# Another order table for a two-block attention and two-expert kernel: the same instructions in another order, some on other engines

## The chip, the cores and the metric

The kernel runs on one core of one Trainium2 chip. The metric is device time in microseconds (us) of one execution. Engines are named as in the profile: PE is TensorE (matmuls; PEld its weight loads), DVE is VectorE, ACT is ScalarE, POOL is GpSimd, SP is SyncE, which issues most DMAs.

## The reference

Rotary attention over 4 batches of 8 heads, 576 positions and 64 columns, and two dense expert layers on the 2304 resulting rows of 512 columns:

```python
q_rot, k_rot = (rotate(q), rotate(k))
scores = scale * np.matmul(q_rot, k_rot.transpose(0, 1, 3, 2))
scores = scores - np.max(scores, axis=-1, keepdims=True)
attn = np.exp(scores)
attn = attn / (np.sum(attn, axis=-1, keepdims=True) + 1e-09)
x = np.matmul(attn, v)                     # to 2304 x 512
...
h = x @ w_in                               # first expert layer, 512 -> 2048 -> 512
g = h * np.clip(h + 3.0, 0.0, 6.0) / 6.0
x = g @ w_out
...
h = x @ w_in                               # second expert layer
P = a[0] + a[1] * h + a[2] * h2 + a[3] * h3
Q = 1.0 + np.abs(b[0]) * np.abs(h) + np.abs(b[1]) * h2
out = (P / (Q + 1e-06)) @ w_out
```

## The kernel before

**Numbers.** Operands of matmuls are split into two 16-bit halves: an upper half (a cast, possibly with a scale) and a lower half (the rest that the cast left off). A product takes three matmuls, upper by upper, upper by lower and lower by upper. So nearly every operand costs a cast and a subtraction or a fused multiply and subtract. Float32 weights are first decoded from the raw bytes (L422 to L427), squared and summed for a scale (L442, L453), and then split (`split16`, L433 and L434, for the first expert; `split_w2`, L1052 and L1053, for the second, whose halves are written over the tile of the weight before them, so that the cast of one weight waits for the second half of the last).

**Attention.** 16 head pairs P0 to P15, four for each batch. `prep_qk` rotates q and k: two products with the sine table (L640), one in place with the cosine table over 1280 columns (L647), two sums (L657), the casts (helper `copy`, L311 on ACT, L313 on POOL, L315 or L317 on DVE) and lower halves (L671), and a DMA transposition (tile `qkt`). A `unit` is 128 rows of queries of both heads of a pair, or the last 64: scores on PE (L704 to L715, tile `s` in PSUM), their row maximum (L719, DVE), a small scalar (L725 or L727), the exponential on ACT (L736), the upper half of P (L757, through `copy`) and the lower half (L758), a DMA transposition, and the product with v on PE (L794).

**First expert.** `layer1` takes 256 rows of one batch at a time, or the 4 x 64 rows left over: PE into PSUM (L899), a gate on ACT and DVE (L906, L908), the upper half of g (`gh`, L910, through `copy`) and the lower (`gl`, L912), and the second matmul (L927).

**Second expert.** `layer2` takes blocks of 512 rows and two of 128 columns of h at a time: PE fills one of two PSUM tiles, `hh` or `hx` (L1151). ACT reads it three times (L1177, L1178, L1179) and DVE twice (L1183, L1184). A chain of further instructions on tiles `lq`, `ls`, `lt` and `lr` gives P / Q, its halves are `lgh` (L1192, ACT) and `lgl` (L1193, DVE), and PE multiplies them with w_out (L1203) into four PSUM tiles `ac`.

**What sets the order.** The function does not emit instructions as it runs: each call of `op` appends an operation with its dependences to a list of 3527, and `Plan.order` then reads the table `ORDER`, a compressed list of numbers. Each number names an operation, the engine that runs it (`"PADGQN"`: PE, ACT, DVE, GpSimd, the SP queue, none) and one of two PSUM banks. Operations are emitted in exactly this order, so each engine's queue, which runs in order, is a subsequence of the table, and semaphore waits between the engines follow from the dependences and from who uses a tile first. The list of engines and the costs given to `op` are not read when a table is there:

```python
for x in code:
    o, e = self.ops[x // 12], "PADGQN"[x % 12 // 2]
    if o.need is not None:
        o.need.bank = x % 2
    ...
    done.add(o.idx)
    result.append((o, e))
```

Of the kernel before, what the change touches and what calls it, by code (L numbers as in the profile page):

```python
# [32 lines left out]
KF = DFF // 128  # L33
# [67 lines left out]
    'PXqjv<`X4ky{$}|ZO2xVXBfA<gSM{FUX01S>FBr3Z<t@8aVTWFAo&~2MWrs-^)r<WD>Io5xu48rbQtsK(3vsh0_$2%o2BE*7jip<@q9~W9^LY^',
    'LWxz$W|fo~%|v7!7RZcNYK{ms5QM6P!G=5qF#G1<hheBqmw6gJy=LL@=?`M6!2;|D=G&f1HUXgo?vc~wK6b8Vx|9&~(;aqE4O<cUu@#e}iTj=%',
    'L_;Y%X*va=kEYlNJW7XQ($g)UIo7d1lo|2O*cSqo9}dGKyG446+5MjUM`_&}dSgAgAqC;CwIhdM$FCpMS(~_eC>>)48$guZ&l#}%aGQ-CkN#p9',
    '&!%I1>gB=U$j@5*W4LEUV3w^OL>b_DXW=vK^MR>@+bo3WDX|KGX9nJEiN6T+#dYX2NAv1nKHeTUb1?6Z9`wQ(>xFu=1K&B`>Y$Hlp9sMZ_C81M',
    'vr^3U*O+L95YLllgX~B2&k#RMu;b9fc5|vQCOSMeLvNnJNb2z3hxu^*c-}7xJ(tZbsl^V%bJ+)<3YNw@OdZCRyO{ZD#E}kn^ZMyUw8qyvAC0|H',
    'dbq*X#Jb(QV7I9&EpW-af(SdK38_ok6MNI7-g<}Mdr#!=A0^-N8AhYFkkp|9cFPOj*EGxCqLN(<v))Kb(F{C)CV5ZOpf&jrzqKS&n#wk89cIK{',
    '$iSX;URX^V@}eAsdc&jmpi8_;rdbzkTS56g-hW()%FPh8b|oDy(FWlJU4dR0g*xL4%D;*2P8j{@G2`A{`z*xGN4iDpK{w`owTQb7`IPn81pS3u',
    '>gd+GHzxeZ&4FEe(yUN=l@|8gtxUBk@0l^L29>E>dNV6BhV|=*psXnGntv#**tL=$RAmd#H!ro&+LRw!l>#MUHYx4qj#;8KDP=Te7b`p(Bj&ho',
    '-rTi1klQAe-vA%PL|#YNVO{C8VzkhX@+fB}lyWfSCTp3^df(aCU`#vhybzzuL;F+-niKlpSw5)uTGkySt_*k`>zQZgP?86&h#6P<B}rE8GS60q',
    'zs8YIi#!{w0_`>$Ivo9l<+xaCpZ2_@{bY_s;J7j93&Ct=!n^2p;9a$v4*g`9e&4dK=f1G%|K&Oja^-jFkC7uZ(r7P8M)I}AO06e3C|9eUv>!P3',  # L110
    'PBTCJJ^hk!<M6q@LIzVh<SNC&b=FA>$*S8U)lwDK=<fk%mM@y`vtDl#T_V?0aizdqS1OUeLvRh2a=SlXN#x~pu~Wh;H<qbTLL^07#Ywbx%QHka',
    'UG<ISpEqkYY|359-0`YtZ7?<99c6E(zst^RyU9LnCK>Twr5D&Uf%}<D2K<fty>KNM`S_IB=AOt5X}tb4Hwe?nPc7^+-0-Q0nY>H|oPi6TD?%ZS',
    'rx!gM{26-t9ms+9w4^Qxk>oGbPp4n9&HNn}{&<G0yZxDYCio(3!0jXtVa*L8zxrXzb29S@%(Ndm5#4#gQ+s(N<Zh9+^t4)>?(*~r7gO)48Pc8P',
    'NcbJRvr*NdH|>WGE$H824-@NdIQ`1og*?_nLeT6l{UA@<a8@!aYLry5Qei5a*Luy5{L*-!K?us|3b`Z=TcxSK&`M(4?Fw8<`0?tcU_-nUd*35=',
    '9#@p-OvYDJ6`|lkEOi#~jf@7Rht<-zEsxv_!&XtCj4j6tgl8g;(0sftu&K@n%h}zoSx0#<^}jr@qz!c|d7qq$A6@&A_DyLaUKTv3wkF1Mwhw~v',
    'fADoFrmiIPU*QOSl^V16_Xlt7U-nHIgZbUbUN~aIG<F<G3qn&G*u2+Bb+9#iD<_p|fo*Rv6@vdp{Ljl>R0owv$iQdqhsXL8Yqkc*(c+H$$JYDo',
    'ZTX5-j{CI9SvIm}<au@x8j+u;#8RgbuN5mQYlQ);TfSq(%sTx??mr7_ZVBn3<0O{lkek50X-9vDJVTkUncqd$Jpt9C1D*D?n1QI>DLu5$p{HOi',
    '*i<gUs1!>Jq}+<JMoALR$TLQvG-Fq3pG^7SCA%Swle2QndM=ixI;DEGCLJXsxF*Uve5=M;pAL%#vZOD8QFu4==icIkf!A(k`t1Slf7v<EXFc&2',
    'I&pD9sz|MQrVrP0=2L_A>!^N3{-VNbuL;g0I|kt#AYKsHx6MM5&6V~q=6~|a$+;n9_NTQbF-SSv-@#Qq;vKVF8MA6^KSXIr85bkSWbM94d^V8p',
    '8mymvnf^@B(CU0@K+T7HnO;i*Be3BtzM*}n5>=|AzfJ#DI?oE6#9`E@N^S8(fbXi1uQ>mNnZKH2urYc|>Sih#WmhrNI(*CizR>1k$HLldbBCco',  # L120
    'm~!8iu(t*7{gki$EcT?lw+gXd<IWPhD9pOe__}zQ3sd@<ID_3eMxQ6Ev{Z77X;1{Wd>X2izjCWGo5*<0So@l<7v`LYqG^8~DuoG`cVw<QB&_w{',
    '$65nDdRPP})p{6DcdK*k0zAg*UQKu8FMr$wi|Gb6Ec`9J%g!X{-`Zh%e8YK=mVCL%qt#PdlUvIAGppVjvO@D{5DLW=T0?4K)(F4#Z2K`@SCe;q',
    '@1Z`38@Ig;sY&0kk?)He9H-pEtd^Us_HkaaXjkCLeq*u%F+2Ln(N`yY{V<%ZwXslTJW3+TN#A8-HFWNScePI^>+~q?l*+ZW#6Y%ULU4h#1s)#o',
    'Pou2USPwLKcN6c^PqQfLh229Ps)B3#ItZVfOEq~ThpVC=2AE_0G$#P%=_>5cC&(o>!k(#-4`xGZqTXMT4#9EX^tKFt;_H_)bj*$#OTMwd;zvcu',
    'uf4!=*Ch9tN7ySw?L1-zA&5w8kQ+Ts@G_m{Rd3-d{`<zUioK^HKg5w&>)9-7u@P2GsJSZ@+d*R@&>gSHoup5(dl&B+`ARYrPX$)UC$P@TWM1V@',
# [1184 lines left out]
```

## Time and profile before

| | |
|---|---|
| time, three runs | 1069.85 us median (1069.81 to 1078.24) |
| the profiled execution | 1069.65 us, of which the span of instructions is 1067.9 us |
| PE busy | 971.1 us, 91% of the span |
| DVE busy | 908.9 us, 85% |
| ACT busy | 738.2 us, 69% |
| POOL busy | 186.2 us, 17% |

The profile is of one execution. Busy times are unions of the engine's instructions; a group's mean is that of its instructions' durations. A stretch of the span is given in us from its start. What an instruction waited for is inferred from semaphore events. Line numbers are those of the kernel before; in the changed kernel they are one higher, as the table has one line more.

### The profile page before, as it was taken

The page shows a single profiled execution, that of the slowest core. Times are in us where ns is not written, and L with a number is a line of the kernel's source. Part 1 is how long each engine was busy: PE and PEld are TensorE (multiplying, and loading weights), DVE is VectorE, ACT ScalarE, POOL GpSimd, SP SyncE. Part 2 cuts the span into 40 slices and gives each one's busy share as a digit, 9 for nine tenths or more (in the row PEclk, how much of TensorE's full clock was granted, in tenths as well). Part 3 has the DMA queues.
Part 4 walks back from the last instruction along what each step waited for, and adds up shares of the span by engine and source line. Part 5 has one row for each costly group of instructions (what it writes and reads, how often), then busy time and mean ns, then how long its engine had stood idle before and what let it go on. Part 6 is the DMA issues. An engine that isn't in the chain of part 4 may idle for free.

```text
span 1067.9 us, 20042 instructions
## 1 busy us (share of the span) xinstructions
PE 971.1 (91%) x7978; PEld 686.2 (64%) x7978; DVE 908.9 (85%) x1389; ACT 738.2 (69%) x1144; POOL 186.2 (17%) x165
## 2 busy tenths in 40 slices
PE   1358799999999999999999989988999999999998
...
PEclk9997799999999999999999999999999999999999
...
GB/s 263 251 223 200 93 120 130 171 152 154 139 162 169 157 147 141 164 106 150 145 80 207 235 165 115 21 40 0 40 41 40 1 39 2 11 1 50 1 20 40
DMA packets 253853, 117.04 MB, mean 110 GB/s; under 512 B 223552, under 2 KB 241088, under 8 KB 253760
## 3 DMA queue, kind: packets, MB, share of 16 engines
...
## 4 chain that ended last, share of the span: by engine, by line
PE 41%; DVE 15%; ACT 7%; issue 3%; POOL 1%; ACTq 0%; DVEq 0%; POOLq 0%
PE h L927 10%; PE ac L1203 10%; PE h L899 8%; PE hx L1151 4%; PE hh L1151 4%; PE h L794 3%; DVE lt L1183 2%; PE s L704 1%; DVE lt L1184 1%; DVE lq L1188 1%; DVE lt L1189 1%; DVE lt L1191 1%; DVE lgl L1193 1%; ACT ls L1178 1%; ACT lq L1177 1%
## 5 line engine op out<-in xcount | busy, mean ns | idle before, releaser
L899 PE MATMUL h<-xt,w 128*128 128x256 f16 x1728 | 199.2, 274 | 5.4 <-DVE t L908 2.8
L927 PE MATMUL h<-gh,w 128*128 128x256 f16 x1080 | 189.1, 273 | 0.0
L899 PEld LDWEIGHTS <-w 128*128 128x128 f16 x1728 | 168.6, 99 | 26.6 <-issue 6.5
L927 PEld LDWEIGHTS <-w 128*128 128x128 f16 x1620 | 156.6, 98 | 18.3
L1203 PE MATMUL ac<-w2o,lgh 128*128 128x512 f16 x516 | 153.4, 379 | 0.5 <-ACT lgh L1192 0.5
L1151 PEld LDWEIGHTS <-w2i 128*128 128x128 f16 x900 | 87.8, 98 | 98.5 <-issue 7.9
L927 PE MATMUL h<-gl,w 128*128 128x256 f16 x540 | 147.2, 273 | 0.0
L736 ACT ACTIVATE e<-s,mx,qal 128x576 f32<-128x576 f32 (+1 forms) x144 | 115.7, 831 | 14.8 <-POOL mx L727 6.1
L719 DVE TENSOR_REDUCE mx<-s 128x2 f32<-128x1152 f32 (+1 forms) x80 | 99.0, 1242 | 5.7 <-PE s L707 4.8
L1151 PE MATMUL hh<-x,w2i 128*128 128x512 f16 (+1 forms) x468 | 100.3, 359 | 2.8 <-DVE y1m L1083 1.4
L1203 PE MATMUL ac<-w2o,lgl 128*128 128x512 f16 x258 | 97.8, 379 | 1.1 <-DVE lgl L1193 1.1
L1151 PE MATMUL hx<-x,w2i 128*128 128x512 f16 (+1 forms) x432 | 91.0, 357 | 6.3 <-DVE lt L1184 3.3
L1203 PEld LDWEIGHTS <-lgh 128*128 128x128 f16 x544 | 53.1, 98 | 64.0 <-issue 1.2
L906 ACT ACTIVATE t<-h,half,d 128x512 f32<-128x512 f32 (+1 forms) x96 | 61.5, 667 | 43.1 <-PE h L899 33.1
L758 DVE TENSOR_TENSOR p<-e,p 128x1152 f16<-128x1152 f32 (+1 forms) x63 | 79.8, 1267 | 7.2 <-ACT p L311 6.1
L794 PE MATMUL h<-v,pt 128*128 128x130 f16 (+3 forms) x1440 | 75.5, 207 | 8.9 <-DVE t L908 3.2
L794 PEld LDWEIGHTS <-pt 128*128 128x128 f16 (+1 forms) x1440 | 71.7, 100 | 14.1 <-issue 13.0
L704 PE MATMUL s<-qkt 64*128 64x512 f16 (+2 forms) x576 | 57.6, 327 | 8.2 <-DMA qkt<-ropea 5.3
L908 DVE SCALAR_TENSOR_TENSOR t<-t,h 128x512 f32<-128x512 f32 x72 | 48.9, 679 | 16.1 <-ACT t L906 16.0
L311 ACT ACTIVATE p<-e 128x1152 f16<-128x1152 f32 (+1 forms) x53 | 58.0, 1093 | 3.0 <-DMA pt<-p 1.4
L424 ACT ACTIVATE raw<-raw,down 128x512 int32<-128x512 uint16 x64 | 48.1, 758 | 14.1 <-DMA raw<-in_moe_w_in_dram 11.4
L1181 DVE SCALAR_TENSOR_TENSOR lq<-ls,kc,lq 128x1024 f32<-128x1024 f32 (+1 forms) x38 | 44.3, 1168 | 12.8 <-ACT lq L1177 9.4
...
## 6 DMA issues: line engine op xcount, KB each, us to landing
...
```

What stands on the lines that cost most here:

```text
L311: act.activation(out, in_, AF.Copy, scale=scale)
L704: pe.matmul(s()[:, a:b], lhsT=kq(1, y, 64 * h, 64 * h + 64)[:, cc * 128:cc * 128 + 128], rhs=kq(0, z, 64 * h, 64 * h + 64)[:, c:c + b - a] ...
L719: op("D", c_dve(n), lambda e: vec.reduce_max(mx()[:, 0, 0:g], sv().rearrange("p (g n) -> p g n", g=g), axis=AX.X, negate=True), r=[s], w=[ ...
L736: act.activation(et()[:, h * (n // g):(h + 1) * (n // g)], sv()[:, h * (n // g):(h + 1) * (n // g)], AF.Exp, bias=mx()[:, 1, h:h + 1], sca ...
L758: op(EN("lo"), c_sub(n), lambda e: EL[e].tensor_tensor(ph()[:, n:2 * n], et()[:, 0:n], ph()[:, 0:n], ALU.subtract), r=es + [(ph, 0)], w=[( ...
L794: pe.matmul(ob()[r0:r0 + m, o:o + k], lhsT=w, rhs=vv[:, 0:k], start=(z == 0 and j == 0), stop=(z == 1 and j == 4))
L899: pe.matmul(hp()[:, o:o + NQ], lhsT=wt[kk]()[:, z, c:c + 128], rhs=x, start=(n == 0), stop=(n == 11))
L906: act.activation(seg(t, c, n), seg(hp, c, n), AF.Relu, bias=half(), scale=x()[:, g:g + 1])
L908: op("D", c_dve(2 * NQ), lambda e, t=t, hp=hp: vec.scalar_tensor_tensor(t(), t(), two(-15), hp()[:, 0:2 * NQ], ALU.min, ALU.mult), r=[hp], ...
L927: pe.matmul(yp()[:, o:o + NQ], lhsT=w[:, s_, m_ * 128:(m_ + 1) * 128], rhs=gt()[:, f], start=(f == 0 and z == 0), stop=(f == KF - 1 and z ...
L1151: pe.matmul(hp()[:, x * n:x * n + n], lhsT=wi[kk]()[:, z, c:c + 128], rhs=xt()[:, kk, y, 0:n], start=(i == 0), stop=(i == 11))
L1203: pe.matmul(accs[j][i]()[0:m], lhsT=g(gt)[:, y * n + x:y * n + x + m], rhs=wt, start=(f == 0 and z == 0), stop=(f == KF - 1 and z == 2))
```

## The change

Only the table `ORDER` differs, from its first line to its last:

```diff
 ORDER = (
-    'c-lo+4NP3wbw2m~&6_umnK8>c6BfCI5K3J{kxLxpP95qZLMU>OMcomllu+UzmpW)m9cmGauBd|?>Jp2k1R<BY6N_$;LtR9Xi!5XjLR@OiTErz5',
...
+    'c-l=^4NP3wbw2m~&CHv}%q%-gX9+=5c0$OCy2v40L|KPW<Pw*<#6k|DQ<qrOK@M`riV|W`hgir(E+GUFmpB9=3n64pE$R@LTGS;Lb%{l-Sv0Yz',
...
 )
```

The operations and their dependences are the same 3527. Of them 131 run on another engine or are issued from another queue: 26 go from DVE to POOL and 21 back, 25 from ACT to DVE and 18 back, 13 from ACT to POOL and 15 back, and some DMA issues change between SP and ACT. Of P's 72 upper halves POOL now casts 13 (9 before), of its 72 lower halves it makes 10 (9 before); of 72 casts of g it makes 23 (29 before), of 72 lower halves of g 16 (14 before). PE's operations all stay on PE, and its order differs mostly by swaps of neighbours.

POOL's queue at the start, from its first computing instruction (the four memsets of v's padding stand before it). `nat` is natural q and k, `ropea` and `gh` the rotation's temporary, `w_5` and its like weights of the first expert, `v_81` and its like halves of v. Before:

```order
L640 TENSOR_TENSOR gh_296<-nat1_99,tab_117 128x20x32
L313 TENSOR_SCALAR w0_5_321<-w1_5_182,wps_307 128x512
L657 TENSOR_TENSOR gl_323<-nat1_99,gh_296 128x2x5x64
L313 TENSOR_SCALAR v91_81<-vnat1_106,qps_220 128x10x64
L313 TENSOR_SCALAR v92_83<-xr_108,qps_220 128x10x64
L313 TENSOR_SCALAR w0_12_570<-w1_12_361,wps_479 128x512
L727 TENSOR_SCALAR mx_554<-mx_554,qal_337 128x2
L313 TENSOR_SCALAR gh_626<-gl_644,qps_220 128x640
L313 TENSOR_SCALAR v93_146<-xt2_110,qps_220 128x10x64
L657 TENSOR_TENSOR rot_826<-nat0_130,ropea_760 128x2x5x64
```

After:

```order
L641 TENSOR_TENSOR ropea_163<-nat0_99,tab_107 128x20x32
L314 TENSOR_SCALAR w0_1_212<-w1_1_102,wps_209 128x512
L314 TENSOR_SCALAR ropea_163<-rot_191,qps_235 128x640
L641 TENSOR_TENSOR gh_275<-nat1_117,tab_107 128x20x32
L314 TENSOR_SCALAR w0_6_302<-w1_6_186,wps_297 128x512
L658 TENSOR_TENSOR gl_327<-nat1_117,gh_275 128x2x5x64
L314 TENSOR_SCALAR v91_121<-vnat1_77,qps_235 128x10x64
L658 TENSOR_TENSOR rot_423<-nat0_99,ropea_347 128x2x5x64
L314 TENSOR_SCALAR gh_275<-gl_327,qps_235 128x640
L314 TENSOR_SCALAR v92_115<-xr_109,qps_235 128x10x64
```

The first pair's product (on `ropea`), a weight's cast and the first pair's cast now stand ahead, where DVE had them, and so do another weight, a further rotation sum and another cast of rotated values; the fifth pair's product of 1280 columns and its sum follow a little later in the same queue.

ACT's queue in the first block of the second expert, at about 695 to 706 us of the profile before. `hh` and `hx` are the PSUM tiles, `w2o10` to `w2o13` weights of w_out, named by the tile that their halves are written to. Before:

```order
L1179 ACTIVATE lt_9396<-hh_9334,cg_8906 128x1024
L1179 ACTIVATE lt_9399<-hx_9261,cg_8906 128x1024
L311 ACTIVATE w2o10_9402<-w2o11_8818,w2qs_9137 128x512
L1178 ACTIVATE ls_9406<-hh_9334,dv_8582 128x1024
L1177 ACTIVATE lq_9408<-hh_9334,cf_8707 128x1024
L1177 ACTIVATE lq_9410<-hx_9261,cf_8707 128x1024
L1178 ACTIVATE ls_9412<-hx_9261,dv_8582 128x1024
L1186 ACTIVATE lr_9478<-lq_9408,qb_7800 128x1024
```

After:

```order
L1180 ACTIVATE lt_9355<-hh_9330,cg_8964 128x1024
L1178 ACTIVATE lq_9357<-hh_9330,cf_8880 128x1024
L1178 ACTIVATE lq_9359<-hx_9256,cf_8880 128x1024
L1179 ACTIVATE ls_9361<-hh_9330,dv_8525 128x1024
L1179 ACTIVATE ls_9363<-hx_9256,dv_8525 128x1024
L312 ACTIVATE w2o11_9371<-w2o12_8931,w2qs_9147 128x512
L1187 ACTIVATE lr_9446<-lq_9357,qb_7951 128x1024
L1180 ACTIVATE lt_9448<-hx_9256,cg_8964 128x1024
```

The three readers of `hh` (here L1178 to L1180, one line higher) are now parted by one instruction alone, and L1180 on `hx` has moved behind the others, a cast and the first reciprocal root.

DVE's queue at the same place. Before:

```order
L1183 TENSOR_TENSOR lt_9396<-lt_9396,hh_9334 128x1024
L1183 TENSOR_TENSOR lt_9399<-lt_9399,hx_9261 128x1024
L1184 SCALAR_TENSOR_TENSOR lt_9396<-lt_9396,cg_8906,hh_9334 128x1024
L1053 SCALAR_TENSOR_TENSOR w2o10_9402<-w2o11_8818,w2qs_9137,w2o10_9402 128x512
L1181 SCALAR_TENSOR_TENSOR lq_9408<-ls_9406,kc_7952,lq_9408 128x1024
L1184 SCALAR_TENSOR_TENSOR lt_9399<-lt_9399,cg_8906,hx_9261 128x1024
L1053 SCALAR_TENSOR_TENSOR w2o11_9420<-w2o12_8912,w2qs_9137,w2o11_9420 128x512
L1181 SCALAR_TENSOR_TENSOR lq_9410<-ls_9412,kc_7952,lq_9410 128x1024
L1053 SCALAR_TENSOR_TENSOR w2o12_9425<-w2o13_8953,w2qs_9137,w2o12_9425 128x512
L1189 SCALAR_TENSOR_TENSOR lt_9396<-lt_9396,cg_8906,lr_9478 128x1024
```

After:

```order
L1184 TENSOR_TENSOR lt_9355<-lt_9355,hh_9330 128x1024
L1054 SCALAR_TENSOR_TENSOR w2o9_9310<-w2o10_8811,w2qs_9147,w2o9_9310 128x512
L1185 SCALAR_TENSOR_TENSOR lt_9355<-lt_9355,cg_8964,hh_9330 128x1024
L1054 SCALAR_TENSOR_TENSOR w2o10_9368<-w2o11_8813,w2qs_9147,w2o10_9368 128x512
L1182 SCALAR_TENSOR_TENSOR lq_9357<-ls_9361,kc_7915,lq_9357 128x1024
L1054 SCALAR_TENSOR_TENSOR w2o11_9371<-w2o12_8931,w2qs_9147,w2o11_9371 128x512
L1182 SCALAR_TENSOR_TENSOR lq_9359<-ls_9363,kc_7915,lq_9359 128x1024
L1054 SCALAR_TENSOR_TENSOR w2o12_9376<-w2o13_8941,w2qs_9147,w2o12_9376 128x512
L1184 TENSOR_TENSOR lt_9448<-lt_9448,hx_9256 128x1024
L1054 SCALAR_TENSOR_TENSOR w2o13_9451<-w2o14_8950,w2qs_9147,w2o13_9451 128x512
L1185 SCALAR_TENSOR_TENSOR lt_9448<-lt_9448,cg_8964,hx_9256 128x1024
L1189 SCALAR_TENSOR_TENSOR lq_9357<-lq_9357,lr_9446 128x1024
```

Before, the first reader of `hx` (L1183) stood among those of `hh`, and its second three rows on. Now both (L1184 and L1185 there) stand behind the lower halves of `w2o10` to `w2o13` and both L1182.

## Rows read from the trace of the kernel before

**Rows 1.** The page: span, PE's busy time, and PE's and its clock's 40 slices.
```profile
span 1067.9 us, 20042 instructions
...
PE 971.1 (91%) x7978; PEld 686.2 (64%) x7978; DVE 908.9 (85%) x1389; ACT 738.2 (69%) x1144; POOL 186.2 (17%) x165
...
PE   1358799999999999999999989988999999999998
...
PEclk9997799999999999999999999999999999999999
```

**Rows 2.** The table by stretches (from:to, length, busy us and instructions, clock, DMA).
```profile
core 0: us, PE busy (x) PEld busy (x) DVE busy (x) ACT busy (x) POOL busy (x), PEclk, DMA share, GB/s
...
81.00:108.00 27.00, 22.72 (x164) 19.60 (x163) 25.46 (x45) 24.66 (x59) 2.25 (x3) 0.79 0.76 211
108.00:135.00 27.00, 22.81 (x172) 18.64 (x173) 21.32 (x38) 21.88 (x40) 3.35 (x5) 0.75 0.31 77
...
189.00:300.00 111.00, 106.48 (x1214) 89.71 (x1212) 105.40 (x161) 82.03 (x132) 28.31 (x22) 1.00 0.66 151
...
600.00:640.00 40.00, 36.32 (x316) 30.72 (x315) 33.63 (x65) 31.21 (x63) 18.10 (x17) 1.00 0.60 190
...
680.00:760.00 80.00, 72.79 (x332) 31.86 (x331) 71.90 (x89) 51.82 (x55) 11.00 (x6) 1.00 0.08 27
...
960.00:1068.00 108.00, 102.12 (x569) 55.25 (x566) 84.74 (x121) 65.97 (x92) 0.00 (x0) 0.99 0.09 27
```

**Rows 3.** Groups of DVE in the first 126 us (count, busy us, mean ns, idle before).
```profile
L647 DVE TENSOR_TENSOR nat<-nat,tab 128x1280 f32<-128x1280 f32 x5 | 7.4, 1486 | 0.0
...
L640 DVE TENSOR_TENSOR ropea<-nat,tab 128x640 f32<-128x640 f32 x6 | 4.9, 820 | 1.1 <-DMA vnat<-in_v_dram 1.1
...
L317 DVE TENSOR_SCALAR ropea<-rot,qps 128x640 f16<-128x640 f32 x5 | 3.2, 638 | 0.0
L317 DVE TENSOR_SCALAR w<-w,wps 128x512 f16<-128x512 f32 x6 | 2.9, 475 | 0.0
```

**Rows 4.** Groups of POOL, then of ACT, over the whole run.
```profile
L640 POOL TENSOR_TENSOR ropea<-nat,tab 128x640 f32<-128x640 f32 x5 | 10.4, 2077 | 10.2 <-DMA qkt<-ropea 10.2
...
L313 POOL TENSOR_SCALAR p<-e 128x1152 f16<-128x1152 f32 x4 | 6.8, 1697 | 26.1 <-ACT e L736 10.2 <-DMA pt<-p 8.0 <-DVE r L842 7.9
...
L313 POOL TENSOR_SCALAR w<-w,wps 128x512 f16<-128x512 f32 x2 | 3.1, 1564 | 9.6 <-DVE wps L401 9.6
...
L311 ACT ACTIVATE p<-e 128x1152 f16<-128x1152 f32 x45 | 52.1, 1159 | 2.1 <-DMA pt<-p 1.4
...
L311 ACT ACTIVATE ropea<-rot,qps 128x640 f16<-128x640 f32 x17 | 13.6, 823 | 2.8 <-DVE rot L657 1.8 <-DVE qps L401 1.0
```

**Rows 5.** The group of DVE's product of 1280 columns over the whole run.
```profile
L647 DVE TENSOR_TENSOR nat<-nat,tab 128x1280 f32<-128x1280 f32 x16 | 25.1, 1569 | 1.5 <-POOL ropea L640 1.4
```

**Rows 6.** The timeline from 28 us (start, us, engine, what; in brackets idle time before).
```profile
28.21 2.03 POOL L640 TENSOR_TENSOR gh<-nat,tab 128x640 f32<-128x640 f32 x1 [26.96 <-DVE w L434]
...
28.78 1.82 DVE L317 TENSOR_SCALAR v<-vnat,qps 128x640 f16<-128x640 f32 x1
```

**Rows 7.** The timeline from 694 us.
```profile
694.90 1.06 ACT L1192 ACTIVATE y<-raw 128x1024 f16<-128x1024 f32 x1 [5.13 <-DVE raw L1191]
...
700.71 1.28 DVE L1184 SCALAR_TENSOR_TENSOR lt<-lt,cg,hh 128x1024 f32<-128x1024 f32 x1
701.89 0.75 DVE L1053 SCALAR_TENSOR_TENSOR w2o<-w2o,w2qs,w2o 128x512 f16<-128x512 f32 x1
702.02 1.11 ACT L1178 ACTIVATE ls<-hh,dv 128x1024 f32<-128x1024 f32 x1 [2.73 <-DVE lt L1184]
...
704.19 2.75 PE L1151 MATMUL hh<-x,w2i 128*128 128x512 f16 x12 [1.34 <-ACT lq L1177]
...
707.52 2.75 PE L1151 MATMUL hx<-x,w2i 128*128 128x512 f16 x12 [0.58 <-DVE lt L1184]
...
708.22 1.66 POOL L313 TENSOR_SCALAR w2o<-w2o,w2qs 128x512 f16<-128x512 f32 x1 [4.78 <-DVE w2o L1053]
...
725.25 5.35 PE L1151 MATMUL hx<-x,w2i 128*128 128x512 f16 x24 [2.72 <-DVE lt L1184]
```

More of the change, by code (lines that the diff above doesn't have):

```diff
@@ L101 @@
[L101 to L125, printed above, removed]
@@ L156 @@
[L156 to L158 removed]
+    'c-l=^4NP3wbw2m~&CHv}%q%-gX9+=5c0$OCy2v40L|KPW<Pw*<#6k|DQ<qrOK@M`riV|W`hgir(E+GUFmpB9=3n64pE$R@LTGS;Lb%{l-Sv0Yz',
+    'MIGw0l=aTS0B?TYoA>VRxx+fC&^+F}dH3A&^PTUUb8AQ$+h96tQEH$DP8u3CC^{Q8E8v=}Gu5iFUx?*ola`Y^*$JqX=gnFcWlPY`#@Le5W@h9b',
@@ new lines @@
+    ')&@E&gk!mDk<p_Rl6>&7Rx<!0cG^)0E15FZ2|Z+%?XV5`IaHXM60z>sEph-f2;nykT8#h%;D^i$wX9pIGFCxTq-+IU$KQI*JF*|5Y{Y(=jj{wx',
+    'C@QqFfH@B>vIeteC0kXxGk#JEmlOph7Mp%DDEAqDGAj8=F$<A7y8@cc5X9N4-6EJ!r8KgTIiQ?p+o-Xhd|vpJ-K?~*2-@F_JBG-5rcNm^H-riE',
+    'taAh!V2y2N&M6*v3WY$8F?j^{sWP4jAv?k})Es>V!^$YDGtaSEIE&wlSPfJ-xL22r$Earo6tQJiPF^UTFtNX*1RbBt{MwK_KEtwuWW#u>G^5N_',
+    '<yb~Does%ZW)(_^aC<gz-6e=XEYpGVwrRT&%*z}MD-San+C=W>!Ty5W?5Z^uGfj?;Oq_&$f!%G{=Ny)n^p(tzBb*5-Lu902akHEZ<edi{t^E6p',
+    '7djl1a=@HoGs+#KO$nJgyPC<UE16+()!BStDOXsX!vnv=z5%PC@7Lr{eLM=LGMy=s-y@3!eF>cnvK?bm928a#I+cs?LK$Ln2c4+nWAup!TA=2Q',
@@ new lines @@
+    'yZ`HfmyV|Fu7BpG25p%QhX?)KX+B}i5K=Jyxa*qLL8eJmcEP_MjMK1Vj&x-EEDbV}Kigis_#yY<)*I*d8riHj0F^JDgnP4+^}-08m3v{zQ~A+W',
+    '+Ml-yF_=cAUG>(!l;kC|NO8iIeLL?1h%gmnq9GD*L)0H-+J5K$*r!K6n({9v%GpqMOI{UUr~wFn#Ptp;L0039COkmB?|}4j^^I>PywD6C;6q9E',
+    '-p+j=G|>gK1}H_G!W5gpcyrun@J;p;I1TR^-32@BBzmX|@5Vo@QO<#t(YU>6F{D?D>f(d!5#-~#NohP=&DQbmhCfa<c(z~d&Cr#D4c3uoeYC1b',
+    'Y)UF~?W7iyPY_YZp-c6_^`xfyVK>?5|Gj-Lgi+^G_=Vwx8YODHa0Ngi<))ALV9BUg<H@&GomING^n0P;`x?x<T2garYqCJiB*E>2QO5OtJFCH*',
+    '*bCd)Cvu&xqQq@EDu2avL#Nn7BFqEfBw|VqW;?}xQj#5$qlbg;4O*P?zzbK5H0x9DlhjYv%_XT9l<W)nU0ge$EFjkU<&)+kqd~bRM_8K<ng%H&',
@@ new lines @@
+    'BA3(3)VeDw)Y#vLJcwtf3?=VJh8xbws=nx$rq$@r_QQZOqLkSuQakPnb6yOIE4Bv;l+C0D3sRW&SPO;+dX#|DcX(M@W;fBp#fJl0kP4Ou&KjLc',
+    'wG_*a8Plp_opvu6Z)V-lA^DKKJOIL3+0r$5#L5hs@B4UNId05rt%n1OU)qpcQ&;3LJ!AO{s`R+VQjb`z;dG42-$Sc3IN>tQNxjQGsbBDUpot{#',
+    'SvSNpA;-(iB(lV5o%@vk)yN5PRS0Iv9h;cF1Nx}@oUp@c4n8e^Rk>%B$@h(ZhYuzU&af*cak<lcRS@|?Mf^V#X6VU`2K5-rMY=6F;8P#WvOa;o',
+    'H2|^f8s3G;_5uIy0ZY3@%I&YwteG#5lRt#d8u`jaamnTwtz`E}FU%mq-bF8$E1mivo001sqfo|tMyG2k)ua@P>vknd+_2_IFmtA`>*H0@XU8)2',
+    'jy{-R!!Rnu(DNCkQ}BQjcN|QWs4BFux>U1k3*W0jmY#S0H06dS^@?3W3P~&(RL{c_M&k@>?#o}<Yw|gFHxSA7Vi0A`u$?!nw$WoM=g=uuo5Jei',
```

84 lines of the change are left out of this document (47 added, 37 removed).

## Prediction

> **What bounds the kernel now.** I read the page first: TensorE (PE) is busy for 971.1 us of a span of 1067.9 us, so 96.8 us in all can be won by order alone, and its matmuls are untouched by the change [rows 1]. The profiled execution took 1069.65 us, 1.75 us more than its span, and stands 0.2 us below the median of 1069.85 us; the sum below is made against 1069.65 us.
>
> Then the table by stretches, to see where PE's idle time lies. The reader is to see two regimes. From 81 to 108 us PE works 22.72 of 27 us while VectorE (DVE) is busy for 25.46 and ScalarE (ACT) for 24.66: there the two engines that prepare operands set the pace. From 189 to 300 us PE works 106.48 of 111 us, so PE sets it, with DVE close behind at 105.40. The late stretches of note are 600 to 640 us (3.7 us idle), 680 to 760 us (7.2 us) and the tail from 960 us (5.9 us) [rows 2]. Up to 135 us the granted clock is also low, 0.79 and 0.75, and the page's clock row shows the same slices [rows 1, 2]; this matters little while PE waits for operands.
>
> It follows that an earlier start of PE's dense part is kept to the end, and that after about 190 us a faster DVE, ACT or GpSimd (POOL) gives something only at a place where PE waits for it by name.
>
> **The change, part by part.** Nothing is added or removed, so the sum has four terms.
>
> *The start, up to the first expert matmul (L899, at 126 us).* Counting along both orders what must be done before it, seven instructions leave DVE for POOL: a rotation product (0.82 us), two weight casts (0.475 each), a cast of rotated q or k (0.64), a rotation sum (priced as the product, 0.82), the product of 1280 columns (1.49) and a small cast (some 0.3) [rows 3]. That is 5.0 us. One cast of 0.64, two small copies and two scalars of a scale come the other way, 1.2 us: DVE is relieved of 3.8 us. ACT is relieved of one cast of 0.82 us and a small copy, 1.1 us together; its other moves cancel [rows 4]. POOL pays much more: 2.08 for the product, as much for the sum, 1.56 for each weight cast, and for the product of 1280 columns, which it never ran, some 4 us as an estimate, twice its product of 640 [rows 4]. With three moves back it is 13 us in all. POOL was idle for most of this stretch (2.25 of 27 us at 81 to 108), so its own queue is no bound [rows 2].
>
> But POOL's work isn't free for DVE. While POOL ran one product of 2.03 us, a DVE cast that normally takes about 0.6 took 1.82 us [rows 6]: 1.2 us lost, 0.6 per microsecond of POOL. That is the upper end. The lower end is nothing, when DVE runs an instruction that isn't disturbed. Between them: the product of 1280 columns takes 1486 ns in the first 126 us and 1569 over the whole run, so the 11 later ones average (25.1 - 7.4) / 11 = 1.61 us, 0.12 more, at a POOL share of 28.31 / 111 [rows 2, 3, 5]. That is 8% of DVE's time for a quarter of POOL's, 0.3 us per microsecond of POOL for instructions of this kind; about half of DVE's time is of such kinds, and I take 0.15. So 13 x 0.15 = 2.0 us are given back: DVE is ahead by 1.8 us, ACT by 1.1. DVE is the fuller of the two, so I take **-1.6 us**; the ends are -3.8 (nothing given back) and -3.8 + 13 x 0.6 = +4.0.
>
> The Trainium skill has a harder rule ("SBUF — State Buffer", section "Who interferes with whom"): GpSimd and VectorE share a port pair under an exclusive lock, and the later of the two waits for the whole of the other's instruction when VectorE reads two operands from SBUF or runs in a two-port mode. The trace agrees only in part, since 1.82 us shows a near full block and an average loss of 0.12 us doesn't; by the rule alone the start would lose, and it is the second rival below.
>
> *The expert and attention stretch, 135 to 600 us.* Most pairs of moves cancel: by group means DVE has 2.8 us less work over the whole program than before, ACT 0.8 us more. What stands on DVE ahead of the scores of the ninth head pair (at 304 us) is 7.3 us less, against 3.8 at the first expert matmul, so the order gives 3.5 us more slack just where DVE was at 105.40 of 111 us. Only a part of PE's 4.5 us of idle time there can go [rows 2]; I take three tenths, **-1.4 us**, with ends -3 and +3, as late halves of P could cost as much as slack gives.
>
> *The first block of the second expert network, 680 to 760 us.* Here I walk the order by the rows. PE fills two PSUM tiles, hh and hx, two matmul groups of 2.6 us each, and can refill one only when five readers are done, three on ACT (L1177 to L1179) and two on DVE (L1183, L1184). The readers of one tile also follow each other: ACT's L1178 on hh waited 2.73 us for DVE's L1184 on hh, though it takes nothing from it. So PE's refill of hh waited 1.34 us, until 704.19, and that of hx 0.58, until 707.52 [rows 7]. Now ACT's three readers of hh come together before DVE's two: from 695.96, when ACT is free, 4.4 us of ACT, 1.22 of DVE, a half of w2o (0.75) and 1.28 end at 703.4. PE's refill of hh is 0.8 us earlier. For hx it turns: DVE now has halves of w2o10, 11, 12 and 13 and two L1181 ahead of its readers of hx. Two halves and two L1181 end at 707.4; w2o12's cast on POOL begins at 706.2 and takes 1.66 [rows 7], its second half ends at 708.6, w2o13 with a cast on ACT at 710.1, and the two readers at 712.6. PE now fills both halves of hh before those of hx; through with hh at 708.8, it waits 3.8 us, and ends its four refills at 718.1 instead of 715.45: 2.6 us lost. The wait of 2.72 us before the refill at 725.25 [rows 7] then shrinks by about half, as PE comes to it later; by the same walk it starts at 726.6. So **+1.4 us**; the ends are -4.6 (the three waits of 1.34, 0.58 and 2.72 gone) and +3.8 (the new wait kept whole).
>
> *The rest of the second expert network.* Blocks of matmuls swap with their neighbours, and POOL has nothing to do. I take 0, with ends -4 and +5 from the 5.9 us of idle time at the tail.
>
> **The sum:** 1069.65 - 1.6 - 1.4 + 1.4 = 1068.05, so **1068.0 us**, no change that can be told: about 1% is what a measurement of this kernel can tell from none.
>
> **The rivals.**
> 1. *The second half gains too.* The start keeps all of -3.8 us, half of the 10.9 us of idle time at 600 to 640 and 680 to 760 us goes, and half of the tail's 5.9: 1069.65 - 3.8 - 5.4 - 3.0 = 1057.4 us. For it: these waits have names, and order can remove them. Against it: the walk above finds a new wait in the worst of these places. Chance 0.17.
> 2. *POOL blocks DVE throughout.* If each of the 13 us costs DVE one, the start moves by -3.8 + 13 = +9.2 us, and with the block's +1.4 the time is 1080.3 us. For it: the 1.82 us [rows 6]. Against it: the mean loss of the late products [rows 3, 5]. Chance 0.08.
> 3. *Slower, by P's halves on POOL.* Six of P's upper halves move onto POOL and two back, at 1.70 us a cast instead of 1.16 on ACT [rows 4], and two lower halves move there and one back. The half's transposition waits for it, PE's product with v waits for that, and everything behind it in PE's order. The price is one POOL instruction of 1.7 and one of 2.0 that stands ahead of it, less the 1.16 of before: 2.5 us; for eight moved halves 20 us, and 1088 us. It decides once a half is later than the slack between it and PE's product. Against it: P's halves are ordered well ahead of those products. Chance 0.05.
>
> **How the numbers follow.** The forecast has the remaining 0.70, with a range of its own from 1061 to 1075 us. Eight times in ten the time should lie between 1058 us, near rival 1, and 1077 us, short of rival 2. Faster by over 1% (below 1059.2) takes most of rival 1, 0.14; slower by over 1% (above 1080.5) takes rival 3 and half of rival 2, 0.09; within 1%: 0.77.
>
> **What would show it.** Right: the first L899 starts 1 to 3 us before 126; POOL is busy for about 200 us; DVE's groups of two operands have longer means; at about 705 to 715 us PE shows a wait of 3 to 4 us for DVE on hx, and none over 1 us on hh before it; PE's idle time from 189 to 300 us is 2 to 5 us. Wrong: the first L899 later than 128 us (rival 2), waits of PE at L794 for POOL (rival 3), or a stretch from 680 to 760 us with under 4 us of idle time (rival 1).

## The result: 0.57% slower, and the profile after

The changed kernel takes **1078.32 us** (median of 20 runs, 1076.23 to 1081.06), the kernel before 1071.19 us (20 runs, 1066.32 to 1078.24): 1.0057 times as long, 95% interval 1.0040 to 1.0074. That is above the predicted range of 1061 to 1075 us, and slower where 1068.0 would have been a little faster. One trace of the experiments below, that of e3, is of a slow run (1087.16 us, left out of its ratio), so only durations from its start are used.

The profiled execution took 1076.6 us. Its page, with span, PE's busy time and the two slice rows of [rows 1]:

```profile
span 1074.8 us, 20039 instructions
...
PE 976.7 (91%) x7972; PEld 692.1 (64%) x7978; DVE 920.1 (86%) x1391; ACT 734.3 (68%) x1139; POOL 187.7 (17%) x168
...
PE   1376899999999999999999989989999999999998
...
PEclk9857799999999999999999999999999999999999
```

The table by stretches of the changed kernel, as [rows 2]:

```profile
core 0: us, PE busy (x) PEld busy (x) DVE busy (x) ACT busy (x) POOL busy (x), PEclk, DMA share, GB/s
0.00:126.00 126.00, 67.34 (x411) 58.76 (x411) 104.17 (x215) 103.56 (x224) 29.19 (x30) 0.78 0.72 208
...
54.00:81.00 27.00, 20.36 (x99) 17.97 (x99) 22.74 (x45) 20.48 (x44) 9.32 (x8) 0.50 0.76 201
81.00:108.00 27.00, 18.61 (x132) 16.24 (x134) 26.36 (x40) 25.34 (x59) 5.45 (x4) 0.74 0.78 215
108.00:135.00 27.00, 23.83 (x179) 20.08 (x175) 23.92 (x49) 23.02 (x47) 4.21 (x5) 0.75 0.46 109
189.00:300.00 111.00, 106.61 (x1213) 90.49 (x1211) 104.49 (x160) 82.23 (x134) 30.51 (x22) 1.00 0.68 153
680.00:760.00 80.00, 74.64 (x339) 33.32 (x339) 71.35 (x91) 50.15 (x55) 10.92 (x9) 0.98 0.08 27
```

Two stretches of the kernel before that were not shown ahead of the prediction:

```profile
0.00:126.00 126.00, 65.18 (x423) 55.37 (x423) 105.84 (x225) 108.45 (x232) 17.98 (x23) 0.89 0.73 209
...
54.00:81.00 27.00, 15.20 (x103) 13.22 (x103) 25.96 (x51) 25.05 (x56) 5.24 (x4) 0.90 0.84 214
```

The stretch to look at is 54 to 81 us. PE is busier than before (20.36 us for 15.20) with slightly fewer instructions (99 for 103), at a granted clock of 0.50, the 1.2 GHz level, while DVE and ACT, the two engines that set the pace here, are less busy (22.74 for 25.96, 20.48 for 25.05); ACT's longest wait there, 4.5 us, is for PE's product with v at L786. Split at the first matmul of each part, the 6.9 us between the two spans lie so:

| part | before | after | difference | predicted |
|---|---|---|---|---|
| start, to the first L899 (L900 now) | 126.3 | 129.5 | +3.2 | -1.6 |
| from there to the second expert's first matmul | 514.8 | 516.9 | +2.1 | -1.4 |
| second expert, to its second block's first matmul | 110.9 | 110.0 | -0.9 | +1.4 |
| from there to the end of the span | 315.9 | 318.4 | +2.5 | 0 |

Each column is one trace, and traces of one order differ: the first L900 comes at 126.3 to 134.3 us in four traces with the old start (before, e1, e11, e12) and at 129.5 to 132.1 in three with the new one (changed, e2, e4). So one trace says little on the first row. The second row is firmer: that part takes 516.7 to 518.8 us in nine traces with the new order there and 514.7 and 514.8 in two with the old start and the old order (before, e8).

### The profile page after: what moved, and what is told of

It reads as the page before. It is cut to its first block, busy times and chain, and to the rows that moved or that the text cites. A ratio compares the mean times of both kernels' runs of the same rounds, so it can differ in the third digit from the quotient of the medians.

```text
span 1074.8 us, 20039 instructions
## 1 busy us (share of the span) xinstructions
PE 976.7 (91%) x7972; PEld 692.1 (64%) x7978; DVE 920.1 (86%) x1391; ACT 734.3 (68%) x1139; POOL 187.7 (17%) x168
## 4 chain that ended last, share of the span: by engine, by line
PE 60%; DVE 23%; ACT 9%; issue 4%; DMA 3%; POOL 1%; SPq 0%; ACTq 0%; DVEq 0%; POOLq 0%
PE h L928 13%; PE ac L1204 12%; PE h L900 10%; PE hh L1152 6%; PE hx L1152 6%; PE h L795 4%; PE s L705 3%; DVE mx L720 2%; PE h L786 2%; DVE gl L913 2%; DMA raw<-in_moe_w_in_dram 2%; DVE p L759 1%; DVE t L909 1%; DVE lt L1184 1%; DVE lt L1185 1%
## 5 line engine op out<-in xcount | busy, mean ns | idle before, releaser
L900 PE MATMUL h<-xt,w 128*128 128x256 f16 x1728 | 198.5, 274 | 7.6 <-DVE t L909 3.8
L900 PEld LDWEIGHTS <-w 128*128 128x128 f16 x1728 | 168.4, 98 | 29.1 <-issue 8.9
L795 PE MATMUL h<-v,pt 128*128 128x130 f16 (+3 forms) x1440 | 75.6, 207 | 4.3 <-DVE t L909 1.4
L795 PEld LDWEIGHTS <-pt 128*128 128x128 f16 (+1 forms) x1440 | 71.6, 100 | 8.9 <-issue 7.6
L425 ACT ACTIVATE raw<-raw,down 128x512 int32<-128x512 uint16 x64 | 48.3, 756 | 17.2 <-DMA raw<-in_moe_w_in_dram 13.4
L312 ACT ACTIVATE p<-e 128x1152 f16<-128x1152 f32 (+1 forms) x51 | 55.2, 1083 | 5.3 <-DMA pt<-p 4.8
L1187 ACT ACTIVATE lr<-lq,qb 128x1024 f32<-128x1024 f32 (+1 forms) x38 | 40.0, 1056 | 21.9 <-DVE lq L1182 21.8
```

The lines of the kernel that those rows point to most:

```text
L312: act.activation(out, in_, AF.Copy, scale=scale)
L795: pe.matmul(ob()[r0:r0 + m, o:o + k], lhsT=w, rhs=vv[:, 0:k], start=(z == 0 and j == 0), stop=(z == 1 and j == 4))
L900: pe.matmul(hp()[:, o:o + NQ], lhsT=wt[kk]()[:, z, c:c + 128], rhs=x, start=(n == 0), stop=(n == 11))
```

## The experiments

"Before" and "changed" are the two tables. A table is cut at an operation, `before[:L900]` being all entries up to it, and `rest(changed)` the entries of the changed table that the first part lacks, in their order. PSUM banks are given anew where the second table's is taken. The ratio is to the kernel before on the same chip, with its interval; each kernel has 6 to 12 runs.

**Which part: e1 to e4.**

```diff
-ORDER = changed
+ORDER = before[:L900] + rest(changed)      e1
+ORDER = changed[:L900] + rest(before)      e2
+ORDER = before[:L1152] + rest(changed)     e3
+ORDER = changed[:L1152] + rest(before)     e4
```

e1:

> The order of before up to the first expert's first matmul (L900 with the numbering of the changed kernel), the changed order behind it. Before ran at 1071.2 us and the changed kernel at 1078.3 (medians of 20). Theory A: most of these 7.1 us are lost in the start, where GpSimd's added work slows VectorE and TensorE's queue puts two products with v ahead of a score; then this kernel takes 1071 to 1074 us and the first L900 starts at about 126 us. Theory B: the start gives its 3 us back, and the loss is made behind it, by the lower halves and casts on GpSimd; then 1076 to 1079 us.

e2:

> The reverse: the changed order up to the first L900, the order of before behind it. Theory A: 1075 to 1079 us, the first L900 at about 129 us. Theory B: 1070 to 1073 us, since a late start is made good later.

e3:

> The order of before up to the second expert's first matmul (L1152, at about 641 us), the changed order behind it, so the second expert alone is new. By the prediction's terms for it (+1.4 and 0): 1071 to 1073 us. Theory C, that the second expert costs what the two traces show from that matmul to the last (418.6 us before, 420.2 after) and the tail more: 1073 to 1075 us. Theories A and B alone: 1070 to 1072 us.

e4:

> The changed order up to the second expert's first matmul, the order of before behind it. Theories A and B: 1077 to 1079 us, all of the loss. Theory C: 1075 to 1077 us. If the two parts add up, this and the run with only the second expert new lie together 7 us above twice the time of before.

Measured: e1 1076.15 us (1.0047, 1.0022 to 1.0071), e2 1077.35 (1.0056, 1.0034 to 1.0077), e3 1073.65 (1.0018, 0.9995 to 1.0041), e4 1079.17 (1.0065, 1.0042 to 1.0089). The start alone costs 6.2 us (A), but all without the start costs 5.0 (B), together more than the whole change. The parts don't add up: what a part costs depends on what it is joined to. Whether the joint of two tables costs time by itself no run tests. Theory C's share is within what can't be told from nothing. So I went on within the start, from e2.

**What in the start: e5 to e8.**

```diff
-15 computing operations of the start on the engines of changed
+the same 15 on the engines of before, at their new places         e5 (from e2)
-PE: ... PV P0 first, PV P0 second, S P1 second ...
+PE: ... PV P0 first, S P1 second, PV P0 second ...                 e6 (from e2)
-ACT: ... L411 DMA raw (the load at 27 us) ...
+SP: ... L411 DMA raw ...                                           e7 (from e2)
-ORDER = before
+ORDER = before, those 15 operations on the engines of changed      e8
```

(S are a unit's scores, PV its product with v.)

e5:

> As the run with only the start new (the changed order up to the first L900, the order of before behind it; 1077.35 us), but the 15 computing operations of the start that changed engine run where they ran before, at their new places in the order. Theory P (GpSimd's added 11 us in the start cost VectorE 5.3 us, which ate what it was relieved of): the start loses less, 1072 to 1075 us. Theory Q (the new order itself, on TensorE's and ScalarE's queues, makes the start late): 1076 to 1079 us, as VectorE then has 7.5 us more to do and 5.3 us less disturbance. First L900 at 126 to 128 us by P, 129 or later by Q.

e6:

> As the run with only the start new, but on TensorE the scores of the second unit of the second head pair (P1) stand ahead of the second of the two products with v, as before; nothing else differs. Theory Q1 (these scores started 8.2 us late behind two products that took 8.7 us at half clock, and the lateness is kept in part): the scores at 70 to 72 us instead of 76, the time 1073 to 1075 us. Theory P or R: 1076 to 1079 us.

e7:

> As the run with only the start new, but one load of a raw weight that ScalarE issues at about 27 us goes to the SP queue, at the same place in the order. Theory R (that issue holds ScalarE for 3.0 us, 0.39 us before, because it now follows four issues of SP closely): ScalarE gets 2.5 us back at 27 us, and the time is 1074 to 1076 us. Theory P or Q1: 1076 to 1079 us.

e8:

> The order of before throughout, but the same 15 operations of the start on the engines that the changed table gives them. Theory P: GpSimd's added work slows VectorE, 1074 to 1078 us, the first L899 at 128 to 131 us. Theory Q: the moves alone are harmless or a gain, 1069 to 1072 us.

Measured: e5 1077.18 us (1.0063, 1.0046 to 1.0080) and e6 1079.19 (1.0067, 1.0041 to 1.0092): no gain, so neither GpSimd's added work (P) nor that place in PE's queue (Q1) is by itself what makes the new start slow. e7 1074.88 (1.0029, 1.0005 to 1.0053): by the ratios of e2 and e7, about half of the loss goes with one load (R). e8 1076.06 (1.0037, 1.0015 to 1.0059): on the old order, the new engines do cost 4 us, as P said, though P's cause isn't shown there: its trace also has the slow products found below.

The load: the timeline of the changed kernel (SPq and ACTq are DMA issues).

```profile
25.82 0.53 SPq L614 DMA_DIRECT2D nat<-in_k_dram  x1
26.39 1.11 SPq L617 DMA_DIRECT2D nat<-in_k_dram  x2
26.86 3.02 ACTq L411 DMA_DIRECT2D raw<-in_moe_w_in_dram  x1
28.08 0.35 SPq L411 DMA_DIRECT2D raw<-in_moe_w_in_dram  x1
29.94 0.77 ACT L425 ACTIVATE raw<-raw,down 128x512 int32<-128x512 uint16 x1 [2.58 <-issue]
34.11 0.75 ACT L425 ACTIVATE raw<-raw,down 128x512 int32<-128x512 uint16 x1 [1.39 <-DMA raw<-in_moe_w_in_dram]
34.15 1.45 SPq L676 DMA_TRANSPOSE qkt<-ropea  x1
```

The same load in the kernel before, also issued by ACT:

```profile
24.54 0.53 SPq L410 DMA_DIRECT2D raw<-in_moe_w_in_dram  x1
24.66 0.39 ACTq L410 DMA_DIRECT2D raw<-in_moe_w_in_dram  x1
```

The issue holds ACT for 3.02 us where SP's issue of a like load takes 0.35. The first pair's transposition follows right behind the landing, and SP's view of waits says so:

```profile
SPq L676 <- DMA raw<-in_moe_w_in_dram: 5.7, 1, 5.7
```

The Trainium skill ("DMA: Bandwidth & Descriptors", section "Issuing engines are not separate DMA queues") says that issuing from several engines saves only the sequencer's time to start a transfer, "usually small relative to the DMA itself". The trace differs in this place: 3.02 us of issue against 7.2 us to landing.

**The load alone, and the middle: e9 to e12.**

```diff
-ACT: ... L411 DMA raw ...
+SP: ... L411 DMA raw ...                                            e9 (from the changed kernel)
+e7 and e5 together                                                  e10
+ORDER = before[:L900] + changed up to L1152 + rest(before)          e11
+e11, 94 computing operations of the middle on their old engines     e12
```

e9:

> The changed kernel with that one load alone moved from ScalarE to the SP queue. Theory R (the held load keeps ScalarE waiting 2.5 us, and the first pair's DMA transposition waits 5.7 us for it to land): 1074.5 to 1076.5 us, 2 to 4 us less than the changed kernel. If a late start is made good later anyway: 1077 to 1079 us.

e10:

> Only the start new, with that load on the SP queue and the 15 computing operations on their old engines; so the new order of the start alone. If GpSimd's part (4 us in the old order) adds to the load's (2.5 us): 1070 to 1072.5 us. If the order itself is what costs the rest: 1074 to 1076 us, as with the load alone moved back (1074.9).

e11:

> Only the middle new: the order of before up to the first L900, the changed order from there to the second expert's first matmul, the order of before behind it. Theory B (the middle costs what is left between all but the start new, +5.0 us, and only the second expert new, +1.9): 1073 to 1075 us. If the second expert holds the loss: 1070 to 1072 us. The prediction's term for this stretch was -1.4 us, which would be 1069 to 1070.

e12:

> Only the middle new, with the 94 computing operations of the middle that changed engine back on their old engines, at their new places. Theory P (GpSimd beside VectorE: from 300 to 600 us VectorE's instructions beside GpSimd take 19.5 us longer than alone, 12.5 before): 1070 to 1072 us. If the new order suits only the new engines: 1074 us or more.

Measured: **e9 1071.58 us (1.0015, 0.9991 to 1.0040)**: one load's queue is worth 6.7 us by the medians and 4.5 by the two ratios, more than expected of it, and the rest of the change can't be told from no change. e9's 12 runs lie in two groups, seven from 1069.97 to 1071.75 us and five from 1074.56 to 1077.32; its median and its trace are of the lower one. e10 1076.20 (1.0042, 1.0020 to 1.0064) and e11 1077.65 (1.0047, 1.0017 to 1.0076) were again slower than their parts promised. e12 1085.53 (1.0132, 1.0098 to 1.0166): taking the 94 moves back makes the new order worse, not better.

**Why one load costs so much: e13, e16 and e17; can the lead be kept: e14 and e15.**

```diff
+for o, e in res:
+    o.fn(e)
+    for _ in range(4 if o.idx == 208 else 0):        # 208 is the load
+        act.activation(junk[:, 0:512], tab()[:, 0:512], AF.Square)   e13 (from e9)
+ORDER = e9[:L900 of batch 1, second half] + rest(before)             e14
+ORDER = e9[:L900 of batch 3] + rest(before)                          e15
-SP: ... L614 and L617 DMA nat (k of the third pair), L411 DMA raw ...
+SP: ... L411 DMA raw, L614 and L617 DMA nat ...                      e16 (from the changed kernel)
-... the load, L428, L435, L435, L672, L672, two transpositions ...
+... L428, L435, L435, L672, L672, two transpositions, the load ...   e17 (from the changed kernel)
```

e13:

> The changed kernel with the load on the SP queue, and where ScalarE issued it four squares of 512 columns that nobody reads (about 0.62 us each, 2.5 us together). So ScalarE is held as long as by the issue, but the load isn't, and the first transposition waits for nothing on ScalarE's DMA queue. If the hold of ScalarE is what costs: 1075 to 1078 us, near the changed kernel (1078.3). If the transposition behind the late load is what costs: 1071 to 1073 us, as with the load moved alone (1071.6).

e14:

> The changed order with the load on the SP queue up to the first matmul of the first expert for the other half of the second batch (at 324 us in the run with the load moved, 3.9 us ahead of before), the order of before behind it. If the lead is kept: 1066 to 1068 us, better than both kernels. If the old order behind it gives the lead up, as it did where the cut lay at the first L900 (1074.9 us): 1070 to 1074 us.

e15:

> The same with the cut at the first matmul for the fourth batch (at 519 us, 2.3 us ahead of before). If the lead is kept: 1067 to 1069 us; if not: 1071 to 1074 us.

e16:

> The changed kernel, the load on ScalarE as there, but SP's load of k for the third head pair, whose three issues run from 25.8 to 27.5 us and beside which ScalarE's issue begins, stands behind SP's next load of a weight. If that neighbour is what holds ScalarE's issue: the issue takes 0.3 to 0.5 us instead of 3.0, and the time is 1072 to 1075 us. If it is held by something else (what is already in flight): 2.5 to 3.5 us again, and 1077 to 1079 us.

e17:

> The changed kernel, but the load that ScalarE issues stands in the program behind the first pair's two DMA transpositions. Every engine's and queue's own order is the same as in the changed kernel; only the wait of the first transposition for this load can fall away. If that wait (5.7 us) is what costs: the transposition starts at about 31 us instead of 34.2, the first scores at about 37, and the time is 1071 to 1074 us, though ScalarE is still held by the issue. If the late weight itself costs: 1077 to 1079 us.

Measured: e13 1072.80 us (1.0011, 0.9990 to 1.0032), so the hold of ACT by itself isn't it. e14 1070.41 (0.9993, 0.9974 to 1.0013) and e15 1074.44 (1.0015, 0.9996 to 1.0034): neither can be told from the kernel before, so no lead is shown to be kept. e16 1077.70 (1.0056, 1.0034 to 1.0077) with an issue of 2.56 us: SP's load of k beside it isn't why the issue is long. e17 1077.85 (1.0060, 1.0040 to 1.0079): the transposition started at 30.68 us and waited for no load, and nothing was gained. So the theory of that wait fell too, and the time is the one named for a late weight.

What e13 and e17 leave of the load is when its weight lands. ACT's decode of that weight (L425) starts at 34.11 us in the changed kernel (shown above), and in e17, e9 and e13, in this order:

```profile
35.74 0.74 ACT L425 ACTIVATE raw<-raw,down 128x512 int32<-128x512 uint16 x1 [2.41 <-DMA raw<-in_moe_w_in_dram]
33.09 0.77 ACT L425 ACTIVATE raw<-raw,down 128x512 int32<-128x512 uint16 x1 [1.83 <-DMA raw<-in_moe_w_in_dram]
33.11 0.76 ACT L425 ACTIVATE raw<-raw,down 128x512 int32<-128x512 uint16 x1
```

SP's later loads of raw weights wait for DVE's L428, which ends the decode of an earlier one (six waits, 9.6 us, from 40 to 66 us of the changed kernel), and the second pair's transposition stands behind them in SP's queue:

| | the weight's decode | a later raw load of SP | the second pair's transposition |
|---|---|---|---|
| changed | 34.11 | 48.06 | 58.95 |
| e17 | 35.74 | 49.17 | 60.03 |
| e9 | 33.09 | 47.00 | 57.41 |
| e13 | 33.11 | 47.05 | 57.47 |

The later the weight, the later the second pair, whether ACT is held (e13) or not. It is so in all traces of the new start: counted from SP's issue of the raw load ahead of it (23.74 us in the changed kernel), the decode starts 10.3 to 11.5 us later in the eight with the load on ACT (e18 below among them) and 8.7 to 9.6 in the six with it on SP. No run moves the landing alone, so this way is what the traces point to, and not shown by a run of its own.

What comes of the lateness I found on PE, at the second pair. In the changed kernel:

```profile
61.88 2.18 PE L752 MATMUL s<-ident,e 128*128 128x128 f32 x9 [0.55 <-ACT e L737]
65.53 1.46 PE L705 MATMUL s<-qkt 64*128 64x512 f16 x9 [1.46 <-DMA qkt<-gh]
66.93 0.50 PE L708 MATMUL s<-qkt 128*128 128x128 f16 x3
67.22 8.74 PE L786 MATMUL h<-vnat,pt 128*128 128x64 f32 x40
75.89 1.46 PE L705 MATMUL s<-qkt 64*128 64x512 f16 x9
```

In e9, the same instructions:

```profile
60.80 2.18 PE L752 MATMUL s<-ident,e 128*128 128x128 f32 x9 [0.55 <-ACT e L737]
63.02 1.47 PE L705 MATMUL s<-qkt 64*128 64x512 f16 x9
64.42 0.37 PE L708 MATMUL s<-qkt 128*128 128x128 f16 x3
64.62 4.63 PE L786 MATMUL h<-vnat,pt 128*128 128x64 f32 x40
69.19 0.83 PE L705 MATMUL s<-qkt 64*128 64x512 f16 x9
```

In the changed kernel PE pauses 1.46 us for the second pair's transposition, and the 40 matmuls behind it (two products with v) take 8.74 us instead of 4.63. The transposes ahead of it (9 in 2.18 us, where nine take 1.15 at 70.12 us of e9) run at the slow pace in both kernels; in e9 the pace rises between the scores and the products, behind the pause it doesn't. So it is in all nine traces with such a pause (1.35 to 2.22 us: the changed kernel, e2, e4, e5, e6, e7, e10, e16, e17): the products ran at the slow pace. Of the ten without it, five ran fast (before, e3, e9, e12, e14) and five slow (e1, e8, e11, e13, e15). Behind the pause the pace stayed slow; without it both occurred. With the load on ACT all seven traces of the new start have the pause; with it on SP two of six have it (e7, e10).

What the slow products hold up is ACT, which copies their result. In the changed kernel:

```profile
76.00 0.28 ACT L312 ACTIVATE xu<-h 128x128 f32<-128x128 f32 x1 [4.54 <-PE h L786]
```

All 14 traces with slow products have such a wait, of 3.5 to 6.4 us; in the five whose products took 4.6 to 5.0 us, and in e18's below, ACT waits for L786 for 0.3 us at most.

**The pause filled: e18.**

```diff
 def mm(e):
+    for j in range(8 if fill else 0):            # only ahead of the second pair's first scores
+        pe.transpose(s()[:, 128 * j:128 * j + 128], fill()[:, 128 * j:128 * j + 128], ident())
     ...
```

> The changed kernel; on TensorE eight more transposes of 128 by 128, whose results are written over, stand ahead of the first scores of the second head pair, where TensorE pauses for 1.5 us. In all nine runs with such a pause the 40 matmuls of the next two products took 8.7 us, in five of ten runs without it 4.6 to 5.0. Theory S (the pause sets TensorE's slow pace for the two products, and that is how a small lateness becomes 4 us): the 40 matmuls take 4.6 to 5.0 us in a good part of the runs, and the time falls to 1073 to 1076 us. If the lateness of the second pair's transposition alone counts: 1077 to 1079 us, as the changed kernel.

Measured: **1074.36 us (1.0023, 1.0000 to 1.0046), 12 runs from 1071.78 to 1076.07**, all below the lowest of the changed kernel's 20. Eight more matmuls make it 4.0 us faster by the medians, 3.6 by the two ratios. In its trace the gap is gone and the products are fast:

```profile
63.41 2.18 PE L759 MATMUL s<-ident,e 128*128 128x128 f32 x9 [0.56 <-ACT e L744]
65.64 1.48 PE L703 MATMUL s<-ident,e 128*128 128x128 f32 x8
67.18 0.83 PE L711 MATMUL s<-qkt 64*128 64x512 f16 x9
67.94 0.34 PE L714 MATMUL s<-qkt 128*128 128x128 f16 x3
68.12 4.63 PE L793 MATMUL h<-vnat,pt 128*128 128x64 f32 x40
```

It is later than e9 at this place by 3.5 us (68.12 for 64.62) and yet more than half of the loss is gone.

## Why the prediction was wrong

**The step that failed** is the term of the start, and in it two sentences. "Nothing is added or removed, so the sum has four terms" priced computing engines alone; the load of a weight by ACT had kept its engine, so it wasn't looked at, though one more of SP's loads, that of k, now stood ahead of it, and its issue grew from 0.39 to 3.02 us. And of the low clock it said: "this matters little while PE waits for operands". In its place the runs showed: with that load on SP, the first L900 starts at 124.0 us in e9 and 124.2 in e14, about 2 us ahead of the kernel before, where -1.6 was predicted, and at 127.2 in e7 and e15, whose products were slow; with it on ACT the second pair's transposition is 1.5 us later than in e9, PE pauses, and two products cost 4.1 us more. While ACT waits for them, DVE and ACT do 3.2 and 4.6 us less work from 54 to 81 us than before. By e18, 4.0 of the 7.1 us (by the two ratios 3.6 of 6.1) hang on the pause and PE's pace behind it. How the load makes the second pair late is shown only in part: holding ACT (e13) and the first transposition's wait (e17) are excluded as the sole cause, and the traces point to the weight's late landing, 1.0 us in the changed kernel against e9, 1.1 in SP's raw load after it. Why ACT's issue is long, and what the other 3 us or so hang on, is open.

**DVE and POOL.** POOL's added work was 11.2 us in the first 126 (29.19 for 17.98), near the predicted 13. What it does to DVE was sized too small, at least in three groups. DVE's groups in the first 126 us of the changed kernel, and of the kernel before (its L640 is in [rows 3]):

```profile
L672 DVE SCALAR_TENSOR_TENSOR ropea<-rot,qps,ropea 128x640 f16<-128x640 f32 x6 | 6.8, 1150 | 0.0
...
L658 DVE TENSOR_TENSOR rot<-nat,ropea 128x640 f32<-128x640 f32 x4 | 5.9, 1468 | 0.0
L641 DVE TENSOR_TENSOR ropea<-nat,tab 128x640 f32<-128x640 f32 x5 | 5.2, 1051 | 0.0
```

```profile
L671 DVE SCALAR_TENSOR_TENSOR ropea<-rot,qps,ropea 128x640 f16<-128x640 f32 x6 | 5.3, 879 | 1.0 <-POOL ropea L313 0.9
L657 DVE TENSOR_TENSOR rot<-nat,ropea 128x640 f32<-128x640 f32 x5 | 4.1, 844 | 0.0
```

Six at 1150 instead of 879 ns, four at 1468 instead of 844 and five at 1051 instead of 820 are 1.6 + 2.5 + 1.2 = 5.3 us, 0.47 for each of POOL's 11.2 us, against the 0.15 that I took and the upper end of 0.6. One pair shows the whole block:

```profile
52.59 1.92 POOL L658 TENSOR_TENSOR rot<-nat,ropea 128x640 f32<-128x640 f32 x1 [8.93 <-DMA raw<-in_moe_w_in_dram]
53.02 2.17 DVE L658 TENSOR_TENSOR rot<-nat,ropea 128x640 f32<-128x640 f32 x1
```

So rival 2 was right in kind, and its sign (the first L900 later than 128 us) came true, but for another reason: with the 15 operations on their old engines the loss stayed (e5), and with the disturbance kept and only the load moved it went (e9). The Trainium skill's rule of the exclusive lock ("SBUF — State Buffer", section "Who interferes with whom") fits single pairs like this one; over the start the three groups give half of it.

**POOL's prices** were too high: the product of 1280 columns took 2.9 us, not 4, P's upper halves of 1152 columns 1.46 us, not 1.70, and POOL was busy for 187.7 us, not 200. The rows of before that I priced by hold two to five instructions, and the same work varies: a weight's cast took 1564 ns in those two and 1031 in four of the changed kernel. Why is not shown. Rival 3 didn't happen; in the changed kernel L795 waited for nothing on POOL.

**The middle, -1.4 predicted, +2.1 measured.** PE's idle time from 189 to 300 us is 4.4 us (111 - 106.61), within the 2 to 5 I named, but so was it before. In e9, which has the lead at its start, the part from L900 to the second expert takes 2.8 us longer than before (517.6 for 514.8), so the lead is given back there. No wait of PE in that part is over 2 us, and e12 gives no sign that the moves are the cause: with them taken back the time rose. Which waits it is, is open.

**The first block of the second expert.** The form was right: the wait of PE for DVE on hx is there, 2.69 us instead of 3.8, and the wait of 1.34 us on hh is gone. (The last line's group is cut off by the end of the window.)

```profile
693.74 5.35 PE L1152 MATMUL hh<-x,w2i 128*128 128x512 f16 x24 [0.71 <-DVE raw L1185]
...
707.57 5.35 PE L1152 MATMUL hh<-x,w2i 128*128 128x512 f16 x24
715.61 7.03 PE L1152 MATMUL hx<-x,w2i 128*128 128x512 f16 x24 [2.69 <-DVE lt L1185]
...
729.67 2.53 PE L1152 MATMUL hx<-x,w2i 128*128 128x512 f16 x11 [1.85 <-ACT lq L1178]
```

The walk had two slips. Its own terms up to the refill of hh add to 703.6, not 703.4; and in the new order the half of `w2o13` stands between the two readers of hx, not ahead of both, as the list of DVE's queue shows. With that put right the walk gives a wait of about 3 us (an estimate from its own terms).

But the new wait took the place of larger ones: the stretch from 680 to 760 us has 5.4 us of idle PE, 7.2 before, and the part to the second block's first matmul is 0.9 us shorter, not 1.4 longer. The waits of PE in this block add to 7.1 us before and 5.2 now: three of 0.90, 0.50 and 1.05 us on its other matmuls, which the walk left out, are gone. The rest lost 2.5 us where I had taken 0 with ends of -4 and +5.
